# A planned attention and feed-forward kernel with batch 0's loads, its global rows and its whole order of work laid out anew

## The chip, the cores and the metric

The kernel runs on one core of a Trainium2 chip. The metric is the device time of one execution in microseconds (us). A core has TensorE (matmuls, into PSUM), VectorE, ScalarE and GpSimd, which work side by side, and SyncE, which here issues most of the loads. Each engine takes its instructions in the order in which the program lists them. In the profile they are called PE (and PEld for its weight loads), DVE, ACT, POOL and SP.

## The reference

Attention over 8 batches of 8 heads, 576 positions and 64 elements, in which each position sees its neighbours up to 32 away, 8 global positions are seen by all and see all; then a feed-forward layer on the 4608 tokens.

```python
scores = scale * np.matmul(q, k.transpose(0, 1, 3, 2))
mask = np.abs(pos[:, None] - pos[None, :]) <= window        # window = 32
mask = mask | is_global[:, None] | is_global[None, :]
scores = np.where(mask, scores, -1000000000.0)
scores = scores - np.max(scores, axis=-1, keepdims=True)
attn = np.exp(scores)
attn = attn / (np.sum(attn, axis=-1, keepdims=True) + 1e-09)
attn_out = np.matmul(attn, v)
x = np.ascontiguousarray(attn_out.transpose(0, 2, 1, 3)).reshape(B * S, H * D)   # 4608 x 512
h = x @ w_in                                                                      # 512 x 2048
g = np.maximum(h, 0.0) + np.log1p(np.exp(-np.abs(h)))
return g @ w_out                                                                  # 2048 x 512
```

## The kernel before

**Jobs and an order.** The kernel doesn't emit its instructions as its loops run. The loops add jobs to a planner (`_Order`, L20): a function that emits the instructions, what it costs on which engine, which jobs it needs, which buffers and PSUM banks it opens and uses. A tuple of some 1,720 numbers, `ORDER` (L335), then says in which order the jobs are placed and on which engine (job number times five plus engine). `run` (L179) goes along it with its own idea of times, gives each PSUM tile one of 8 banks and emits the jobs sorted by the planned start. The order that a job has on its engine is thus written out beforehand; the chip keeps to it and waits where a planned time isn't met. The planner's model has a wait of TensorE for its own instructions, in blocks of 256 with the first after 442 (`ASK`, `NEED`, `SLOW`, L38 to 41, `stall`, L44), and a rule for the port that VectorE and GpSimd share: a VectorE job marked `port` waits for the GpSimd job that is running (`self.other`, L217), a GpSimd job for the VectorE job of that kind (`self.mine`). Where TensorE would stand still for 0.7 us or more in the first 34 us, `keep` (L135) puts filler matmuls (L704, tile `warm`).

**Loads.** For batches 0 and 1, `add_parts` (L744) loads queries (w = 0) and keys (w = 1) in three pieces each, natural layout, on SP's queue: two of 256 positions (t = 0, 1) and a tail of 64 (t = 2, `FULL`). Each piece is cast to bf16, transposed by TensorE into PSUM (`tr`, L808), with matmuls beside it that pick out the global positions (tile `pick`), and copied out (`trev`, L833). Both halves of a piece share one PSUM tile. `fill` and `gev` (L865, L870) copy the picked keys and queries. Later batches are loaded whole (`load_qk`), cast, transposed by VectorE, and picked by matmuls (L849, L862). V comes in two halves of 4 loads each (`load_v`, L443), cast into `vb`. The first product's weights are loaded as four chunks by GpSimd's queue (L1304), between its casts. SP loads batch 1 after a marker that reads the second of these chunks (`follow`, L726), and V of batch 1 after one that reads the second chunk of the second product's weights. Those are issued by GpSimd (L1308) once its job `landed` (L1385) has copied an element of the last query piece of batch 1.

**Global rows.** Per batch, `sg` (L923) makes the scores of the 8 global queries against all keys, `mx` the maxima of both halves of the heads (L942, L943), `gexp` the exponentials (L949), `tpg` (L954, L956) their transposes, `ov` (L965) the product with V in 72 small matmuls into two PSUM tiles in turn. `odd` copies one of them to SBUF, `both` adds the other and takes the reciprocal of the sum, `gv` scales the result into `vg` for the values.

**Pairs, values, feed-forward.** The 36 `pairs` of 4 blocks of 32 positions are scored (`sc`, L1040), masked (in PSUM by a matmul for the first four, `mk` for the first two, else by VectorE, L1044), reduced to maxima (L1055, L1057), shifted (`sub`, L1063, on GpSimd or VectorE), exponentiated (L1076, L1080), summed (L1087, L1089), normalised (`no`, L1095, on GpSimd or VectorE) and transposed by VectorE (`tp`, L1104, tile `pt`). `val` (L1207, tile `xo`) multiplies with V. Four pairs make one of 9 tiles of 512 tokens (the first tile comes in three parts, the second in two) for the feed-forward layer: `first` (L1242, tile `h`), softplus (L1248), `second` (L1253, tile `o`), copy and store.

## Time and profile before

| | |
|---|---|
| time, median of 3 runs | 341.49 us (340.54 to 342.74) |
| time of the profiled execution | 342.18 us |
| its span, first to last instruction | 340.5 us |
| instructions | 12210 |
| busy TensorE, VectorE, ScalarE, GpSimd | 94%, 76%, 68%, 50% |
| moved by DMA | 42.74 MB |

A row of a timeline has the start in us from the begin of the span, the time in us, engine, line, operation, the tile written and the tiles read, shapes and count, and in brackets how long the engine stood idle before it and what ended that. "issue" is a wait for which the profile shows no releaser. A group has its busy time, the mean ns of one, and the idle time before its instructions. Of TensorE's time, "busy" counts overlapping matmuls once but includes the drain of each. A row of waits has who waited for whom, us in total, how often, and the longest. A row of a window has its length, then the busy time and the number of instructions of PE, PEld, DVE, ACT and POOL, the granted TensorE clock as a share of the full one, the busy share of the DMA engines and GB/s.

### The profile page before, as it was taken

What the parts mean: (1) busy time and instruction counts of PE and PEld (TensorE: products, weight loads), DVE (VectorE), ACT (ScalarE), POOL (GpSimd) and SP (SyncE); (2) the same over time, 40 slices, a digit from 0 to 9 for tenths busy, and PEclk for the clock granted to TensorE, in tenths of its full rate; (3) what the DMA queues carried; (4) which work ended last, traced back from release to release, by engine and by line L of the source; (5) the groups of instructions that cost most, each with busy time, mean ns of one, the idle gap of its engine ahead of it and who ended that gap; (6) DMA issues with size and microseconds to landing.
All of it is one profiled execution on the core that took longest, in us unless ns stands there. A gap on an engine that the chain in (4) does not pass through costs nothing.

```text
span 340.5 us, 12210 instructions
## 1 busy us (share of the span) xinstructions
PE 319.2 (94%) x5333; PEld 169.4 (50%) x5333; DVE 259.4 (76%) x409; ACT 230.0 (68%) x469; POOL 169.1 (50%) x155
## 2 busy tenths in 40 slices
PE   6787899988999999999799999999999989999996
PEld 3435785555555454544354445444544444445443
DVE  7598679994999799979999999799985979061000
ACT  5688789975687866489638583769466746765442
POOL 5464457863695789608375328644532431460000
PEclk9679999999999999999999999999999999999999
DMA  7999499979799999999950997008111020002003
GB/s 193 220 173 244 123 162 191 175 142 192 127 171 211 174 204 185 189 151 231 164 132 34 173 165 177 2 2 171 36 56 39 33 97 2 31 31 96 0 0 123
DMA packets 168733, 42.74 MB, mean 126 GB/s; under 512 B 153192, under 2 KB 165736, under 8 KB 168680
## 3 DMA queue, kind: packets, MB, share of 16 engines
q1 hardware_dynamic: 160664, 28.33, 47.4%
q0 software_dynamic: 6144, 10.49, 13.2%
q10 hardware_dynamic: 1872, 3.15, 2.5%
q8 instruction: 41, 0.67, 0.9%
q14 instruction: 12, 0.10, 0.1%
HBM read 36.71 MB, written 9.44 MB: 136 GB/s over the span
## 4 chain that ended last, share of the span: by engine, by line
PE 41%; DVE 23%; SPq 11%; POOL 7%; DMA 7%; issue 6%; ACT 4%; POOLq 0%; DVEq 0%; ACTq 0%
PE h L1242 19%; PE o L1253 15%; SPq L440 7%; SPq L445 4%; DMA stage<-in_q_dram 4%; DVE sm L1087 4%; PE xo L1207 3%; POOL pn L1095 3%; DVE st L1044 2%; DMA stage<-in_v_dram 2%; POOL st L1063 2%; PE s L1040 2%; DVE gm L942 2%; DVE m L1057 2%; DVE pn L1095 2%
## 5 line engine op out<-in xcount | busy, mean ns | idle before, releaser
L1253 PE MATMUL o<-wout,g 128*128 128x512 bf16 (+1 forms) x592 | 137.4, 374 | 0.0
L1242 PE MATMUL h<-xT,win 128*128 128x512 bf16 (+3 forms) x768 | 135.8, 326 | 0.4 <-DVE xT L696 0.2
L1248 ACT ACTIVATE g<-h 128x512 bf16<-128x512 f32 (+3 forms) x192 | 85.5, 501 | 44.8 <-PE h L1242 43.7
L1242 PEld LDWEIGHTS <-win 128*128 128x128 bf16 x768 | 67.3, 98 | 60.3 <-issue 1.2
L1253 PEld LDWEIGHTS <-g 128*128 128x128 bf16 x592 | 55.3, 98 | 60.7 <-ACT g L1248 1.3
L1063 POOL TENSOR_TENSOR st<-st,m 128x1024 f32<-128x1024 f32 x27 | 51.9, 1931 | 49.4 <-DVE m L1057 49.3
L1095 POOL TENSOR_TENSOR pn<-st,rs 128x1024 bf16<-128x1024 f32 (+1 forms) x29 | 51.4, 1783 | 48.5 <-DVE rs L1089 46.4
L1044 DVE TENSOR_TENSOR st<-s,mask 128x512 f32<-128x512 f32 x64 | 41.5, 676 | 12.0 <-PE s L1040 12.0
L1087 DVE TENSOR_REDUCE sm<-st 128x8 f32<-128x1024 f32 x32 | 38.3, 1197 | 8.6 <-ACT st L1080 8.6
L1057 DVE TENSOR_REDUCE m<-st 128x8 f32<-128x1024 f32 x32 | 38.4, 1207 | 0.4
L1080 ACT ACTIVATE st<-st 128x1024 f32<-128x1024 f32 x32 | 32.9, 1057 | 1.1 <-POOL st L1063 1.0
L1104 DVE STREAM_TRANSPOSE pt<-pn 128x512 int32<-128x512 int32 x36 | 24.6, 690 | 3.9 <-POOL pn L1095 3.6
L696 ACT CAST xT<-xo 128x512 bf16<-128x512 f32 (+3 forms) x31 | 12.9, 476 | 17.9 <-PE xo L1207 17.9
L696 ACT COPY osb<-o 128x512 f32<-128x512 f32 (+1 forms) x29 | 16.6, 577 | 11.1 <-PE o L1253 9.8
L1095 DVE TENSOR_TENSOR pn<-st,rs 128x1024 bf16<-128x1024 f32 (+1 forms) x11 | 19.9, 1818 | 0.1
L696 POOL CAST kb<-stage 128x1152 bf16<-128x1152 f32 (+2 forms) x12 | 14.4, 1218 | 8.1 <-DVE rs L1089 5.1
L949 ACT ACTIVATE pg<-sg,gnb 128x320 bf16<-128x320 f32 (+1 forms) x32 | 14.9, 575 | 5.0 <-DVE gnb L943 5.0
L693 POOL TENSOR_SCALAR qb<-stage 128x1152 bf16<-128x1152 f32 (+2 forms) x10 | 12.9, 1286 | 10.7 <-DMA stage<-in_v_dram 7.3
L1248 ACT ACT_TABLE_LOAD x13 | 16.7, 1283 | 0.5 <-PE h L1242 0.3
L1040 PE MATMUL s<-kx,qx 64*32 64x128 bf16 x1152 | 15.4, 224 | 1.3 <-DVE qx L789 0.6
L696 POOL CAST vb<-stage 128x1152 bf16<-128x1152 f32 x11 | 12.6, 1145 | 7.2 <-DMA stage<-in_v_dram 5.5
L1265 POOL DMA_DIRECT2D out_dram<-osb x24 | 14.0, 584 | 3.7 <-DVE osb L696 3.7
(124 smaller groups left out, 313.2 us busy)
## 6 DMA issues: line engine op xcount, KB each, us to landing
stage<-in_v_dram SPq DMA_DIRECT2D x64, 144.0 KB, 4.6
stage<-in_k_dram SPq DMA_DIRECT2D x48, 144.0 KB, 3.8
stage<-in_q_dram SPq DMA_DIRECT2D x48, 144.0 KB, 3.6
out_dram<-osb POOLq DMA_DIRECT2D x24, 256.0 KB, 3.2
out_dram<-osb ACTq DMA_DIRECT2D x11, 256.0 KB, 2.1
stage<-in_k_dram SPq DMA_DIRECT2D x4, 512.0 KB, 9.1
stage<-in_q_dram SPq DMA_DIRECT2D x4, 512.0 KB, 6.2
win<-in_moe_w_in_dram POOLq DMA_DIRECT2D x4, 512.0 KB, 6.9
```

Source lines behind the costliest of these rows:

```text
L440: eng.dma_start(out=stage[w][quad(r), :, e, :], in_=SRC[w][b, HG * g:HG * g + HG].rearrange("a (c i e) (f d) -> e f i (a c) d", i=BL, e=2, ...
L696: {"ACT": nc.scalar.copy, "DVE": V.tensor_copy, "POOL": nc.gpsimd.tensor_copy}[e](out, in_)
L1044: V.tensor_tensor(out=PS["st", n][:, h, :, :], in0=PS["s", n, h][:, :, :], in1=mask[:, h, j0:j0 + PB, :, :].rearrange("p j s i -> p j (s i ...
L1057: V.reduce_max(out=m[:], in_=flat(PS["st", n], h0, h1), axis=AX)
L1063: on(e).tensor_tensor(out=t, in0=t, in1=over(PS["m", n, y][:], SL * BL), op=OP.subtract)
L1080: nc.scalar.activation(out=t, in_=t, func=AF.Exp)
L1087: V.reduce_sum(out=sm[:], in_=flat(PS["st", n], h0, h1), axis=AX)
L1095: on(e).tensor_tensor(out=PS["pn", n][:, :, :, h0:h1].rearrange("p x s h -> p h x s"), in0=PS["st", n][:, h0:h1], in1=PS["rs", n, y][:].re ...
L1104: V.transpose(out=bass.AP(base.tensor, base.offset, ap=[list(base.ap[0]), [2 * STEP, PB // 2], [STEP + BL // 2, 2], [1, SL * BL]]), in_=PS ...
L1242: nc.tensor.matmul(out=h[:, :], lhsT=w_in_t[c // 4][:, kd, c % 4 * P:(c % 4 + 1) * P], rhs=PS["xT", m][:, kd, lo:hi], start=(kd == 0), sto ...
L1248: nc.scalar.activation(out=PS["g", m, c][:, lo:hi], in_=PS[key][:, lo_of(c, hi - lo)], func=AF.Softplus)
L1253: nc.tensor.matmul(out=PS["o", m, ns, a][:, :], lhsT=PS["g", m, kf][:, ns * P:(ns + 1) * P], rhs=w_out_t[kf // 4][:, kf % 4, a:z], start=( ...
```

## The change

The list of batch 0's pieces is written with the queries ahead; the global rows of batch 0 are reduced and exponentiated by halves of the heads, and their product with V goes into one PSUM tile, so that the copy and the sum of two are gone; each transposed half piece has a PSUM tile of its own; the marker ahead of the second product's weights reads the query tail of batch 1; the planner's port rule and several of its costs are changed; and `ORDER` is a new sequence.

```diff
-    SLOW = ((30000, 9300), (37000, 6500), (51000, 7300), (62000, 6500), (250000, 5600), (1e9, 4200))
+    SLOW = ((28000, 10700), (38000, 6700), (62000, 6500), (80000, 7200), (150000, 6200), (250000, 5800), (1e9, 4300))
+    def issue(self, j):
+        return j["moves"] or j["port"] == 2
+    def freed(self):
+        t = self.other[1]
+        for n, e in self.given[1:] if self.given else ():
+            if e != "POOL":
+                continue
+            j = self.jobs[n]
+            at = None if self.issue(j) or any(d["end"] is None for d in j["deps"] + j["behind"]) else self.due(j)
+            if at is None or at > t + 100:
+                break
+            t += j["cost"]["POOL"][0]
+        return t
-                    elif e == "DVE" and j["port"] and self.other[0] <= t + 100:
-                        t = max(t, self.other[1])
-                    elif e == "POOL" and not j["moves"]:
-                        t = max(t, self.mine)
+                    elif e == "DVE" and j["port"] and self.other[0] <= t + 100 and self.other[1] > t:
+                        t = self.freed()
+                    elif e == "POOL" and not self.issue(j) and t >= self.mine[0] - 1:
+                        t = max(t, self.mine[1])
...
     ORDER = (
-        42, 107, 121, 126, 47, 52, 92, 116, 9, 236, 221, 225, 240, 87, 132, 137, 83, 14, 251, 255, 97, 143, 102, 268,
+        24, 42, 47, 52, 83, 4, 191, 121, 126, 107, 92, 208, 195, 210, 102, 298, 111, 19, 97, 132, 137, 29, 116, 152,
...
-    FIRST = ([(0, 0), (1, 0), (1, 1), (1, 2), (0, 2), (0, 1)], [(0, 0), (1, 0), (1, 1), (1, 2), (0, 2), (0, 1)])
+    FIRST = ([(0, 0), (0, 2), (0, 1), (1, 0), (1, 2), (1, 1)], [(0, 0), (1, 0), (1, 1), (1, 2), (0, 2), (0, 1)])
...
-            if e == 0:
-                PS["tr", b, w, t] = psum(("tr", b, w, t), [P, 2, HG, P], BF16)
-            ps = PS["tr", b, w, t]
+            ps = PS["tr", b, w, t, e] = psum(("tr", b, w, t, e), [P, HG, P], BF16)
...
-                for y in range(2):
+                for y in range(2 if b else 1):
                     PS["ov", b, y] = psum(("ov", b, y), [P, 2 * D + 1], FP32)
...
-            t = PS["odd", b]
-            V.tensor_tensor(out=t[:], in0=PS["ov", b, 0][:, :], in1=t[:], op=OP.add)
+            t = PS["odd", b] if b else PS["ov", 0, 0]
+            if b:
+                V.tensor_tensor(out=t[:], in0=PS["ov", b, 0][:, :], in1=t[:], op=OP.add)
...
-        heads = ((0, 1),)
+        heads = ((0, 1),) if b else ((0,), (1,))
...
-            job = o.add({"POOL": (1040, 1040), "DVE": (1000, 1080)} if n < TP else {"POOL": (1905, 1905), "DVE": (1130, 1210)}, lambda e, y=y: no(e, y), [job], rank=at,
+            job = o.add({"POOL": (1040, 1040), "DVE": (650, 730)} if n < TP else {"POOL": (1905, 1905), "DVE": (1130, 1210)}, lambda e, y=y: no(e, y), [job], rank=at,
...
-            T["landed"] = o.add(pool(100), lambda e: nc.gpsimd.tensor_copy(seen[:, 0, :], natural(0, 1)[:, 0, 0, 0, 0:1]), [T["part", 1, 0, FULL]], rank=0)
+            T["landed"] = o.add(pool(100), lambda e: nc.gpsimd.tensor_copy(seen[:, 0, :], natural(0, FULL)[:, 0:1]), [T["part", 1, 0, FULL]], rank=0)
```

In the new sequence SP's first loads are: the key tail of batch 0, its first query piece, its two key pieces, the query tail, the second query piece, V, then two key pieces of batch 1, the marker for the first weights, and the rest of batch 1 with its last query piece at the end. TensorE's list has 22 filler matmuls instead of 29, none of them between the global row of batch 0 and the pairs behind it. On VectorE stand 4 normalisations and 9 subtractions of the later pairs (before: 8 and 5), on GpSimd the others.

60 lines of the change are left out of this document (33 added, 27 removed), and 142 rows, old and new, of the table ORDER.

## The prediction

> **What bounds the kernel now.** I read the page first, then who waited for whom, then the chain of waits, and last the timelines of the stretches that these pointed at.
>
> ```profile
> PE 319.2 (94%) x5333; PEld 169.4 (50%) x5333; DVE 259.4 (76%) x409; ACT 230.0 (68%) x469; POOL 169.1 (50%) x155
> PE   6787899988999999999799999999999989999996
> DVE  7598679994999799979999999799985979061000
> PEclk9679999999999999999999999999999999999999
> ```
>
> TensorE is the engine that is never far from busy, but VectorE stands at nine tenths in most slices from the 7th to the 30th, so attention is paced by VectorE, and TensorE fills up with the feed-forward matmuls. How much of TensorE's time is work shows in the two groups of the feed-forward part and one stretch of the chain in which they run with no wait:
>
> ```profile
> L1253 PE MATMUL o<-wout,g 128*128 128x512 bf16 (+1 forms) x592 | 137.4, 374 | 0.0
> L1242 PE MATMUL h<-xT,win 128*128 128x512 bf16 (+3 forms) x768 | 135.8, 326 | 0.4 <-DVE xT L696 0.2
> ...
> 294.33 4.10 PE o L1253 x19
> ```
>
> 19 matmuls in 4.10 us are 0.216 us each. Both products have 576 full matmuls' worth of columns (36 or 144 groups by the loops), 1152 in all, so 1152 x 0.216 = 249 us of the span cannot be ordered away. What is left, some 91 us, is attention's own matmuls, the start, and waits. The change leaves the matmuls of both products as they are, so it can only move the last two. The waits of TensorE that name a releaser are led by two VectorE results, the transposed probabilities and the transposed global rows:
>
> ```profile
> PE xo L1207 <- DVE pt L1104: 3.4, 3, 1.6
> PE ov L965 <- DVE pgt L956: 3.2, 4, 2.0
> ```
>
> **The order and the port.** Behind those two lines stand VectorE instructions that take far longer than others of their kind. First VectorE, then GpSimd in the same stretches, then TensorE just behind them:
>
> ```profile
> 68.16 2.67 DVE L1095 TENSOR_TENSOR pn<-st,rs 128x1024 bf16<-128x1024 f32 x1
> 158.50 5.75 DVE L1095 TENSOR_TENSOR pn<-st,rs 128x1024 bf16<-128x1024 f32 x1
> 179.83 1.30 DVE L1095 TENSOR_TENSOR pn<-st,rs 128x1024 bf16<-128x1024 f32 x1
> 183.41 4.35 DVE L696 CAST vb<-stage 128x1152 bf16<-128x1152 f32 x1
> 189.53 0.75 DVE L696 CAST vb<-stage 128x1152 bf16<-128x1152 f32 x1
> 273.14 2.51 DVE L1095 TENSOR_TENSOR pn<-st,rs 128x1024 bf16<-128x1024 f32 x1
> ```
>
> ```profile
> 157.87 1.52 POOL L693 TENSOR_SCALAR qb<-stage 128x1152 bf16<-128x1152 f32 x1
> 159.28 3.79 POOL L1063 TENSOR_TENSOR st<-st,m 128x1024 f32<-128x1024 f32 x2
> ...
> 183.81 1.91 POOL L1063 TENSOR_TENSOR st<-st,m 128x1024 f32<-128x1024 f32 x1
> 185.65 1.49 POOL L696 CAST kb<-stage 128x1152 bf16<-128x1152 f32 x1
> ```
>
> ```profile
> 72.22 0.38 PE L1207 MATMUL xo<-pt,vg 32*64 32x384 bf16 x8 [1.63 <-DVE pt L1104]
> 169.34 0.80 PE L965 MATMUL ov<-vb,pgt 32*32 32x129 bf16 x72 [1.97 <-DVE pgt L956]
> 277.28 0.40 PE L1207 MATMUL xo<-pt,vg 32*64 32x448 bf16 x8 [1.23 <-DVE pt L1104]
> ```
>
> The same normalisation takes 1.30 us alone and 5.75 us while GpSimd runs three instructions without a pause; it ends 1.2 us after the last of them. The V cast that takes 0.75 us alone ends after GpSimd's second instruction. The excess is 1.37 + 4.45 + 1.21 us on the three normalisations and 3.60 us on the cast, 10.6 us of VectorE, and TensorE waits 1.63 + 1.97 + 1.23 = 4.83 us right behind the three. The old plan lets a VectorE job of this kind wait only for the GpSimd job that is running at that moment (`other`); the new one (`freed`) counts the whole run of GpSimd jobs that are due behind it, which is what the rows show. So the new sequence is laid out with the price that these rows have. It doesn't avoid the exposure: by the instruction lists, VectorE still has 13 normalisations and subtractions of the later pairs (8 and 5 before, 4 and 9 after) and 8 instead of 10 of the later casts. I take three fifths of the 4.83 us: **-2.9 us**, between -4.8 (all gone) and +1.0 (one new collision of the size of the last). Without a collision, the next to arrive at these places is the exponential or the score matmul that feeds the same chain, for which I leave the other two fifths.
>
> The Trainium skill (SBUF — State Buffer, "Who interferes with whom") says that VectorE and GpSimd share one port pair under an exclusive lock, held "for the whole instruction" by whichever starts first. By that the 5.75 us would have been one GpSimd remainder of 0.89 us and 1.30 us of its own, and the cast at 183.41, which started before GpSimd's at 183.81, would not have waited. The rows differ: VectorE got in only when GpSimd had nothing more queued. By the page `freed` would count too much, and this term would shrink to about -1.
>
> **The start.** The words of the change promise that batch 0's queries are loaded ahead of its keys. The list of loads does not show it: `ORDER` overrides `FIRST`. Before: keys 0, keys 1, queries 0, key tail, query tail, queries 1. After: key tail, queries 0, keys 0, keys 1, query tail, queries 1. The first four are the same bytes, so they are in at the same time; what differs is what follows them.
>
> ```profile
> 11.83 0.42 PE L823 MATMUL tr<-ident,kb 64*64 64x64 bf16 x8 [1.04 <-POOL kb L696]
> 13.31 0.29 PE L1040 MATMUL s<-kx,qx 64*32 64x128 bf16 x2
> 18.48 0.68 PE L932 MATMUL sg<-kx,qg 64*32 64x320 bf16 x16 [0.76 <-DVE qg L696]
> 19.10 2.90 PE L704 MATMUL warm<-pgt 128*128 128x512 bf16 x7
> 28.88 0.25 PE L1207 MATMUL xo<-pt,vg 32*64 32x128 bf16 x4 [1.49 <-issue]
> 30.17 3.73 PE L1242 MATMUL h<-xT,win 128*128 128x128 bf16 x64 [0.20 <-DVE xT L696]
> ```
>
> ```profile
> 10.55 0.76 POOL L615 TENSOR_SCALAR mask<-near 128x144 bf16<-128x144 f32 x2 [0.95 <-DVE mask L611]
> 11.38 0.40 POOL L696 CAST kb<-stage 128x256 bf16<-128x256 f32 x1
> ...
> 24.19 0.80 POOL L1304 DMA_DIRECT2D win<-in_moe_w_in_dram  x1
> ```
>
> ```profile
> win<-in_moe_w_in_dram POOLq DMA_DIRECT2D x4, 512.0 KB, 6.9
> ```
>
> Before, the key tail stood on GpSimd behind the mask (10.55 + 0.76), so its transposes began at 11.83 and the first scores at 13.31. After, it is cast ahead of the mask, and the mask is finished at about the same time, so the first scores can start some 0.5 us sooner. The queries' last transposes now stand ahead of the second pair's scores, so that the global row (18.48) can follow those scores at once: some 1.5 us sooner. The path then reaches the issue wait at 28.88. The kernel's planner books such waits at TensorE's 442nd instruction and every 256 after it, each released some 10 us after the instruction 312 places earlier; for the 698th, which is the one at 28.88, that is the 386th, the end of the global row, so this wait moves with it. But the first feed-forward matmuls (30.17) need all four weight chunks, the last of which is issued at 24.19 and, at the page's median of 6.9 us to landing (its last column), is in at about 31, and ScalarE has eight exponentials to do whatever their order. I take **-1.0 us**, between -2.0 and 0.
>
> ```profile
> 24.42 0.60 DVE L696 COPY odd<-ov 64x129 f32<-64x129 f32 x2
> 25.66 0.28 DVE L982 TENSOR_TENSOR odd<-ov,odd 128x129 f32<-128x129 f32 x1
> ```
>
> One sum for batch 0's global rows drops these, 0.88 us of VectorE ahead of the first values. The issue wait up to 28.88 hides them: **0 us**, and if that cover goes, up to -0.9. The maxima by heads add one reduction and let the exponential start on half a row; a bank for each turned piece adds no instruction and holds PSUM banks until its copy is done: both 0, and I let neither be worth more than those 0.9 us, lost or gained.
>
> **The weights of the second product.** Their loads stand on GpSimd behind a marker (`landed`): so far a copy out of batch 1's last query piece, now one out of its query tail.
>
> ```profile
> 35.06 0.61 POOL L696 CAST kb<-stage 128x512 bf16<-128x512 f32 x1 [0.70 <-DMA stage<-in_k_dram]
> 41.02 0.23 POOL L1385 COPY seen<-stage 128x1 f32<-128x1 f32 x1 [3.33 <-DMA stage<-in_q_dram]
> ```
>
> ```profile
> 75.97 4.53 DMA stage<-in_q_dram
> ...
> 82.90 0.46 PE L849 MATMUL pick<-qb,pick 128*32 128x128 bf16 x18 [1.02 <-POOL qb L693]
> ```
>
> The marker waited 3.33 us at 41.02; without that, and with batch 1's keys issued before the marker of the first weights instead of behind it, these weights start 3 to 6 us sooner. SP's queue stands behind them, up to the query load that ends TensorE's wait of 1.02 us at 82.90. That wait goes: **-1.0 us**, at most -1.0; it gains nothing more, since TensorE has feed-forward work there.
>
> **Sum.** The profiled execution took 342.2 us (span 340.5). -2.9 - 1.0 - 1.0 = -4.9 gives 337.3; the median of the runs lies 0.7 under the profiled one, so 336.6 us. The rest of the new sequence, whose waits the old trace can't show, I take at 0 and put into the range.
>
> **Rivals.**
> *The collisions move instead of going.* The plan's times drift from the chip's by some tenths of a microsecond per step, and 13 exposed instructions are left. For it: the old sequence was planned with a port rule too, and has four collisions. Against: that rule ignored the queue behind. Then only the start and the load are gained, and one new wait of 1 us comes: 342.2 - 2.0 + 1.0 - 0.7 = 340.5 us.
> *The clock stays low.*
>
> ```profile
> 11.35:21.59 10.24, 8.71 (x138) 4.25 (x139) 8.12 (x17) 7.57 (x31) 5.86 (x8) 0.50 1.26 186
> ```
>
> From 11.35 to 21.59 the granted clock was 0.50, and it came back under the seven filler matmuls of 19.10. After, these stand only ahead of the first values. If the clock comes back behind the 64 feed-forward matmuls, their 3.73 us become up to 7.5 and the gain of the start is lost: 336.6 + 3.7 = 340.3 us. For it: TensorE was busy 8.71 of those 10.24 us and still slow. Against: the same seven fillers stand just ahead of these 64. The Trainium skill (TensorE: Matmul & The Clock Gate, "Part 1: The HAM clock gate") has the full clock come after about 3.4 us of sustained work; by that rule the clock should have risen well before 21.59, which this row does not bear out.
> *Early keys push the first weights back: slower.* In the new list SP issues two of batch 1's key pieces behind V, ahead of its marker for the first weights; before, the two went out here, and SP's issue itself was held up for 5.31 us:
>
> ```profile
> 26.40 5.31 SPq L490 DMA_DIRECT2D stage<-in_k_dram  x2
> ```
>
> Those two pieces took until 35.06 and later to arrive, with the weights on the other queue. If the weights yield instead, the last chunk is some 4 to 5 us later, near 35.5. It decides from the moment when the 10th of the 16 first groups needs that chunk, about 31.3: 4.2 us of waiting, the gain of the start gone, no later cover, and the collisions of the next 40 us laid out for other times: 342.2 + 4.2 - 0.7 = 345.7 us. Against it: the key rows waited for the weights, not the reverse. The Trainium skill (DMA: Bandwidth & Descriptors, "Queues, rings and completion order") has each DMA engine alternate between queues packet by packet, which is this rival's mechanism; the 8.7 us from 26.40 to 35.06 speaks more for the weights going first.
>
> **Chances.** Forecast 0.55, moved collisions 0.26, low clock 0.07, weights pushed back or another new wait of that size 0.12. About 1% (3.4 us) is what a measurement can tell here. Under 338.1 us lie most of the forecast's cases (0.48) and few of the rest (0.03): faster 0.51. Over 344.9 us lie the last rival and a tail of the second (0.15). Between: 0.34. The forecast alone runs from 332.5 (every term at its lower end, and 1 us of further waits gone) to 339.5; eight in ten over all cases from 332.5 to 343.5, which leaves out most of the last rival.
>
> **What would show it.** Right, if VectorE's normalisations and V casts have no member over 2 us, the waits of TensorE for pt and pgt fall to 3 us together, the first 64 feed-forward matmuls start before 29.5 us, and the marker is copied before 37 us. Wrong, if the granted clock is 0.50 past 28 us, if TensorE waits for the first weights, or if new waits of 2 us stand in the chain beyond 100 us.

## The result, and the profile after

| | before | after |
|---|---|---|
| median of the runs, us | 341.61 (4 runs, 340.54 to 342.74) | 350.63 (4 runs, 349.16 to 351.72) |
| profiled execution, us | 342.18, span 340.5 | 349.62, span 347.9 |
| mean granted TensorE clock | 0.985 | 0.975 |

The ratio is 1.0246, with a 95% interval of 1.0206 to 1.0286: 8.4 us slower by the ratio (9.0 by the medians), where 5 us faster was forecast. The page of the changed kernel:

```profile
PE 314.6 (90%) x5278; PEld 171.5 (49%) x5326; DVE 263.2 (76%) x418; ACT 226.0 (65%) x455; POOL 170.1 (49%) x156
...
PEclk9669999999999999999999999999999989999999
...
win<-in_moe_w_in_dram POOLq DMA_DIRECT2D x4, 512.0 KB, 9.9
```

TensorE's share went from 94 to 90%. (48 of its matmul records are missing here, 5278 beside 5326 weight loads, so counts of matmuls in this one trace run a little low.) The clock row has an 8 late in the span, where before had only 9s there. The weights of the first product took a median of 9.9 us to land, before 6.9. SP's queue and its first loads:

```profile
1.25 1.37 SPq L510 DMA_DIRECT2D stage<-in_k_dram  x2
2.67 0.60 SPq L506 DMA_DIRECT2D stage<-in_q_dram  x1
...
16.33 3.25 SPq L506 DMA_DIRECT2D stage<-in_k_dram  x2
```

The two loads of the key tail went first, so the first large piece was issued at 2.67 us, before at 1.27. At 16.33 batch 1's two key pieces go out, just when GpSimd issues the weights. TensorE in order of time (the bracket is the wait ahead of a row, and what ended it):

```profile
14.47 0.63 PE L1061 MATMUL s<-kx,qx 64*32 64x128 bf16 x32
...
19.51 0.38 PE L1055 MATMUL s<-mask,ident 128*128 128x512 bf16 x1 [1.05 <-ACT st L1097]
22.59 0.58 PE L1055 MATMUL s<-mask,ident 128*128 128x512 bf16 x1 [2.71 <-DVE rs L1110]
...
32.64 1.74 PE L1263 MATMUL h<-xT,win 128*128 128x128 bf16 x28 [0.64 <-DMA win<-in_moe_w_in_dram]
35.56 1.74 PE L1263 MATMUL h<-xT,win 128*128 128x128 bf16 x28 [1.18 <-DMA win<-in_moe_w_in_dram]
...
87.84 0.35 PE L863 MATMUL pick<-qb,pick 128*32 128x128 bf16 x12 [1.46 <-DVE qb L707]
...
246.23 1.02 PE L1228 MATMUL xo<-pt,vb 32*64 32x32 bf16 x100
249.65 0.22 PE L1228 MATMUL xo<-pt,vb 32*64 32x64 bf16 x4 [2.41 <-issue]
...
276.52 0.42 PE L1061 MATMUL s<-kx,qx 64*32 64x128 bf16 x32
279.09 1.03 PE L980 MATMUL ov<-vb,pgt 32*32 32x129 bf16 x72 [2.16 <-DVE pgt L970]
```

The first scores come at 14.47 instead of 13.31. The second bank of the fourth pair's scores is that of a turned query piece whose copy VectorE makes only at 21.82, hence the 2.71 us. The weights hold TensorE twice. Far behind that stand two waits that before did not have: 2.41 us inside a run of value matmuls, ended by nothing that the profile shows ("issue"), and 2.16 us for `pgt` at the last global product. What made the second shows on VectorE and GpSimd:

```profile
266.50 3.75 POOL L1116 TENSOR_TENSOR pn<-st,rs 128x1024 bf16<-128x1024 f32 x2 [4.54 <-DVE rs L1110]
270.19 1.33 POOL L1286 DMA_DIRECT2D out_dram<-osb  x2
271.52 1.16 POOL L712 CAST vb<-stage 128x1152 bf16<-128x1152 f32 x1
...
269.06 1.80 DVE L712 CAST vb<-stage 128x1152 bf16<-128x1152 f32 x1
270.78 2.98 DVE L1084 TENSOR_TENSOR st<-st,m 128x1024 f32<-128x1024 f32 x1
...
278.58 0.45 DVE L970 TENSOR_REDUCE pgt<-own 128x288 bf16<-128x288 bf16 x1
```

VectorE's V cast (0.75 us alone) and its subtraction end 0.6 and 1.1 us after GpSimd lets go, at 270.25 and 272.68. The subtraction waited through two output stores and a cast. All of pgt's chain stands behind it. The windows behind the two waits (PE busy and its count first, the granted clock third from the right):

```profile
246.83:250.24 3.41, 1.00 (x112) 0.87 (x103) 0.24 (x1) 0.12 (x1) 1.89 (x1) 1.00 0.05 12
...
277.55:280.96 3.41, 1.53 (x74) 1.12 (x76) 2.96 (x7) 0.78 (x3) 2.88 (x2) 0.76 0.23 82
280.96:284.37 3.41, 3.41 (x13) 1.25 (x11) 1.03 (x4) 1.55 (x3) 0.87 (x1) 0.74 0.16 59
```

TensorE is busy 1.00 and 1.53 of 3.41 us. The clock of 0.76 and 0.74 is one stretch that lies across both windows: from 279.3 to 282.7 us the granted clock was 0.50. Before, every window from 240 us on had 1.00.

### The profile page after: what moved, and what is told of

The parts are those of the page before. It is cut to its first block, busy times and chain, and to the rows that moved or that the text cites. A ratio compares the mean times of both kernels' runs of the same rounds, so it can differ in the third digit from the quotient of the medians.

```text
span 347.9 us, 12155 instructions
## 1 busy us (share of the span) xinstructions
PE 314.6 (90%) x5278; PEld 171.5 (49%) x5326; DVE 263.2 (76%) x418; ACT 226.0 (65%) x455; POOL 170.1 (49%) x156
## 4 chain that ended last, share of the span: by engine, by line
PE 63%; DVE 16%; issue 6%; DMA 5%; SPq 4%; POOL 4%; ACT 2%; DVEq 0%; POOLq 0%
PE h L1263 29%; PE o L1274 25%; DVE st L1065 4%; PE xo L1228 3%; DMA win<-in_moe_w_in_dram 3%; DVE m L1078 3%; POOL pn L1116 2%; PE s L1061 2%; DVE sm L1108 2%; SPq L461 2%; DMA stage<-in_v_dram 2%; DVE st L1084 1%; PE ov L980 1%; SPq L510 1%; SPq L506 1%
## 5 line engine op out<-in xcount | busy, mean ns | idle before, releaser
L1274 PE MATMUL o<-wout,g 128*128 128x512 bf16 (+1 forms) x553 | 130.4, 375 | 3.7 <-issue 2.9
L1116 POOL TENSOR_TENSOR pn<-st,rs 128x1024 bf16<-128x1024 f32 (+1 forms) x33 | 60.7, 1848 | 82.5 <-DVE rs L1110 74.0
L1084 POOL TENSOR_TENSOR st<-st,m 128x1024 f32<-128x1024 f32 x23 | 43.4, 1896 | 37.3 <-DVE m L1078 37.2
L1065 DVE TENSOR_TENSOR st<-s,mask 128x512 f32<-128x512 f32 x64 | 40.8, 677 | 10.9 <-PE s L1061 10.8
L712 DVE CAST xT<-xo 128x512 bf16<-128x512 f32 (+3 forms) x23 | 11.9, 558 | 13.2 <-PE xo L1228 13.2
L712 ACT CAST xT<-xo 128x512 bf16<-128x512 f32 (+3 forms) x25 | 11.0, 487 | 14.4 <-PE xo L1228 14.4
L1061 PEld LDWEIGHTS <-qx 64*32 64x32 bf16 x1152 | 10.6, 92 | 15.5 <-issue 14.1
L1084 DVE TENSOR_TENSOR st<-st,m 128x1024 f32<-128x1024 f32 x9 | 17.1, 1911 | 0.1
L1228 PE MATMUL xo<-pt,vb 32*64 32x96 bf16 (+2 forms) x1328 | 14.2, 210 | 2.4 <-issue 2.4
```

Of the source, the lines that this page charges most:

```text
L712: {"ACT": nc.scalar.copy, "DVE": V.tensor_copy, "POOL": nc.gpsimd.tensor_copy}[e](out, in_)
L1061: nc.tensor.matmul(out=PS["s", n, g][quad(a ^ g), x, :], lhsT=qx[b % 2][rows(g), a, j * BL:(j + 1) * BL], rhs=kx[b % 2][rows(g), a, e0 * B ...
L1065: V.tensor_tensor(out=PS["st", n][:, h, :, :], in0=PS["s", n, h][:, :, :], in1=mask[:, h, j0:j0 + PB, :, :].rearrange("p j s i -> p j (s i ...
L1084: on(e).tensor_tensor(out=t, in0=t, in1=over(PS["m", n, y][:], SL * BL), op=OP.subtract)
L1116: on(e).tensor_tensor(out=PS["pn", n][:, :, :, h0:h1].rearrange("p x s h -> p h x s"), in0=PS["st", n][:, h0:h1], in1=PS["rs", n, y][:].re ...
L1228: nc.tensor.matmul(out=PS["xo", v_, hd // 2][hd % 2 * D:(hd % 2 + 1) * D, (x - X0) * BL:(z - X0) * BL], lhsT=lhs, rhs=rhs, start=start, st ...
```

## The experiments

Each ratio is to the kernel before, run on the same chip in turn with it. The old kernel's own median moved from 341.02 to 342.73 us between the sets of runs, so two rows are better compared by their ratios than by their medians, and a difference of two ratios has the uncertainty of both. Where an expectation names a wait of 2.37 us, it counts the whole gap beyond the usual step between two matmuls; the row's bracket has 2.16 for the same one. The edits that move work use a helper on the finished list of jobs: `behind(a, b)` puts job a right behind job b, `behind(a, b, 0)` right ahead of it; an engine's own instructions keep their order otherwise.

| run | median, us | ratio (95% interval) |
|---|---|---|
| the change | 350.63 | 1.0246 (1.0206 to 1.0286) |
| e1 marker first | 352.57 | 1.0304 (1.0242 to 1.0367) |
| e2 old kernel, early keys | 340.91 | 0.9960 (0.9922 to 0.9999) |
| e3 turned piece early | 350.92 | 1.0256 (1.0197 to 1.0314) |
| e4 key tail second | 349.47 | 1.0220 (1.0156 to 1.0284) |
| e5 global product later | 347.41 | 1.0167 (1.0084 to 1.0250) |
| e6 six matmuls ahead | 349.48 | 1.0211 (1.0144 to 1.0277) |
| e7 four edits of the start | 351.27 | 1.0249 (1.0177 to 1.0322) |
| e8 e5, e6 and e7 | 346.66 | 1.0119 (1.0055 to 1.0183) |
| e9 e4, e5, e6 and two fills | 346.65 | 1.0178 (1.0145 to 1.0212) |
| e10 GpSimd's cast first | 347.31 | 1.0207 (1.0173 to 1.0242) |
| e11 old kernel, covers | 340.21 | 0.9972 (0.9937 to 1.0007) |
| e12 old kernel, early keys and covers | 339.01 | 0.9948 (0.9919 to 0.9977) |
| e13 new code, old order | 340.94 | 0.9965 (0.9930 to 0.9999) |
| e14 new start, old rest | 360.93 | 1.0531 (1.0466 to 1.0596) |
| e15 old start, new rest | 343.83 | 1.0057 (1.0016 to 1.0098) |
| e16 seven more fillers | 346.34 | 1.0120 (1.0036 to 1.0205) |
| e17 e13, early keys and covers | 341.94 | 0.9964 (0.9916 to 1.0012) |
| e18 e15 and e5 | 342.61 | 1.0001 (0.9963 to 1.0038) |

### The first theory: early keys push the weights back (e1, e2)

The new trace showed the slower rival of the prediction at work to the letter: the last weight chunk landed at 35.51 us. So the first two runs took it out of the new kernel and put it into the old.

```diff
-                if x == 0 and b:
+                if b and (w, t) == (1, 0):
                     follow(0, w_in_t[1])
```

> The changed kernel, with the marker of the first weights put ahead of batch 1's first key piece again, so that no key load of batch 1 starts before the weights. Theory A (the early keys push the first weights back, and TensorE's wait for them is most of the loss of 9 us): the last chunk of w_in lands by about 32 us instead of 35.5, the waits of TensorE for win (1.8 + 2 + 1.2 by the trace) go, and the time falls by 3 to 4 us, to about 347. Theory B (the late copy of a turned piece, with the half clock, costs the start 2 to 2.5 us) and C (the key tail's loads at the head of SP's queue cost 1.2 to 1.4 us): less than 1 us either way, because the feed-forward matmuls then wait for something else. Theory D (the loss is in the rest of the sequence): less than 1 us either way.

```diff
+    behind(T["part", 1, 1, 0], T["part", 1, 0, 0], 0)
+    behind(T["part", 1, 1, 1], T["part", 1, 0, 0], 0)
```

> The kernel before, with batch 1's first two key pieces put ahead of the marker of the first weights, as the changed kernel has them; nothing else moves. Theory A: the chunks of w_in land 3 to 5 us later than at 21.6 to 30.7, TensorE waits for them, and the time rises by 3 to 4 us, to about 345. Theories B, C and D, which put the loss elsewhere: within 1 us of 341.6, since the key rows were not on TensorE's path.

e2 refutes it. e1 gained nothing either, but it is the weaker test: in its trace the last chunk still landed at 34.26 us, since GpSimd issued it behind a normalisation that waits for VectorE. TensorE's waits for the weights fell from 1.8 to 0.5 us all the same, and a new wait of 1.6 us for `pt` stood right behind. e2's page and its row on TensorE show that the mechanism is real:

```profile
win<-in_moe_w_in_dram POOLq DMA_DIRECT2D x4, 512.0 KB, 10.6
```

```profile
31.81 4.45 PE L1242 MATMUL h<-xT,win 128*128 128x128 bf16 x40 [3.40 <-DMA win<-in_moe_w_in_dram]
```

The weights landed in a median of 10.6 us instead of 6.9, and TensorE waited 3.40 us. Yet the time did not rise. By the trace's records the 129th matmul of the first product started at 50.1 us instead of 47.0, but the 321st at 108.7 instead of 108.0: the lag of 3.1 us shrank to 0.7, because the old kernel's waits for its queries (1.02 us at 82.90) and for `pt` at 71 us (1.63, in e2 0.51) took it up.

### Bank and queue head (e3, e4), and four edits of the start (e7)

```diff
+    behind(T["turn", 0, 0][1][0], T["gev", 0])
```

> The changed kernel, with the copy out of one turned piece of the queries (the one whose bank the fourth pair's second half waits for, at 21.8 us) put ahead of the first sum of the global rows on VectorE. Theory B: the waits of 1.05 and 2.71 us of the fourth pair's mask matmuls go, and the time falls by about 2 us, to 348.6. Theory A: the feed-forward matmuls still wait for the weights that come at 35.5 us, so less than 0.7 us is gained. Theories C and D: less than 0.7 us.

```diff
+    behind(T["part", 0, 1, 2], T["part", 0, 0, 0])
```

> The changed kernel, with the loads of batch 0's key tail issued behind the first query piece instead of at the head of SP's queue. Theory C: the first query piece is issued at about 1.3 us instead of 2.67, the first scores start 1.2 us sooner than 14.5, and the time falls by about 1.2 us. Theory A: the start is sooner by that much, but the feed-forward matmuls wait for the weights all the same, so less than 0.5 us of it reaches the end. Theories B and D: less than 0.5 us.

e3 took the 2.71 us from the mask matmuls and met it again as a wait of 3.10 us at the first global product:

```profile
19.14 0.59 PE L1055 MATMUL s<-mask,ident 128*128 128x512 bf16 x2 [1.05 <-ACT st L1097]
...
23.18 2.14 PE L980 MATMUL ov<-vb,pgt 32*32 32x129 bf16 x72 [3.10 <-ACT st L1097]
```

e4 did what theory C said: first scores at 12.99 us, and 1.2 us sooner by the records all the way to 225 us; the span fell by 1.4 us. The ratio fell by 0.0026 (0.9 us), which the intervals do not separate from none. Then the edits together, with the last weight load ahead of the normalisations (it is `o.jobs[15]`, the load before it `o.jobs[14]`):

```diff
+    behind(T["turn", 0, 0][1][0], T["gev", 0])
+    behind(T["part", 0, 1, 2], T["part", 0, 0, 0])
+    behind(o.jobs[15], o.jobs[14])
-                if x == 0 and b:
+                if b and (w, t) == (1, 0):
```

> The changed kernel with four edits of the start together: batch 1's first keys behind the marker of the first weights, the key tail's loads behind the first query piece, the turned piece copied out early, and the last of the four weight loads issued on GpSimd ahead of the two normalisations instead of behind them. Theory S (weights, bank and head of SP's queue hide one another, so that each edit alone gains little): the last chunk of w_in lands by 32 us, TensorE waits under 1 us for win, the first feed-forward matmul starts by 29.5 us, the 129th by 49.5 instead of 52.8, and the time falls by 3 us or more. Theory L (what is gained there is lost again in the following 40 us): the 129th is early, but the time falls by less than 1.5 us.

```profile
30.84 3.73 PE L1263 MATMUL h<-xT,win 128*128 128x128 bf16 x64 [0.47 <-ACT xT L712]
36.86 0.32 PE L1228 MATMUL xo<-pt,vg 32*64 32x256 bf16 x8 [2.29 <-DVE pt L1125]
```

The 64 matmuls now run without a wait for weights, whose last chunk landed at 32.02. Then 2.29 us for `pt` stand where the weights stood, and the "issue" wait at 49 us grew to 2.5. Nothing was gained, as in theory L, and sooner than it has it: the 129th matmul of the first product, which both theories put early, started at 54.8 us (52.8 in the change). Several chains that end close together at 36 us are the likely reason; no run shows it by itself.

### The two late waits (e5, e6, e10) and e8

Job 1463 is the last global product, the others are second-product matmuls that stand behind it; in e6 job 1300 is the value matmuls at 246 us; in e10 job 1458 is GpSimd's cast, 1426 the normalisation ahead of its stores.

```diff
+    for n in (1352, 1353, 1369, 1370, 1372, 1373, 1374, 1375, 1376, 1377):
+        behind(o.jobs[n], o.jobs[1463], 0)
```

> The changed kernel, with ten matmuls of the second product that stand right behind the last global product on TensorE put ahead of it, four of them from the two groups that are open. Theory D1 (the late wait of 2.37 us for pgt at 276.7, which a subtraction of 2.98 us and a V cast of 1.80 us on VectorE make, and the half clock of 3.4 us that follows it, are 2.4 to 4 us of the loss): the wait falls to under 0.7 us, no window of half clock stands at 279, and the time falls by 2 to 4 us. Theory D0 (TensorE is not on the path there; the ten matmuls were done in time anyway): within 0.7 us. What happens before 270 us stays as it is.

```profile
276.54 2.11 PE L1274 MATMUL o<-wout,g 128*128 128x512 bf16 x9 [0.16 <-issue]
278.58 0.80 PE L980 MATMUL ov<-vb,pgt 32*32 32x129 bf16 x72
```

The wait is gone, the product takes 0.80 us instead of 1.03, and the window from 277.55 has the clock at 1.00: theory D1. The medians are 3.2 us apart, the ratios 0.0079 (2.7 us), and their intervals still overlap.

```diff
+    for n in (1180, 1198, 1181, 1182, 1199, 1200):
+        behind(o.jobs[n], o.jobs[1300], 0)
```

> The changed kernel, with six matmuls of the second product that stand behind the value matmuls at 246.1 us put ahead of them. Theory F (the wait of 2.41 us at 249.65, for which no semaphore is late, is TensorE's own instruction stream: in every trace such a wait stands at the same count of matmuls and weight loads, 8641 here, and ends 8.8 to 9.1 us after the 312th before it): the wait stays at the 8641st, so six value matmuls earlier in their run, ends at the same time, and shrinks by about 1.2 us, to 1.2; the time falls by 1.2 us, more if a half clock behind it goes. Theory N (it is a hidden wait of those value matmuls for data): the wait stays between the same two value matmuls.

```profile
247.21 0.98 PE L1228 MATMUL xo<-pt,vb 32*64 32x32 bf16 x94
249.33 0.24 PE L1228 MATMUL xo<-pt,vb 32*64 32x96 bf16 x9 [1.14 <-issue]
```

94 value matmuls instead of 100 ahead of the wait, and 1.14 us instead of 2.41: theory F in both its numbers. The wait keeps its place in the count of instructions, not among the data. The median fell by 1.2 us, within the noise; 0.90 us came back at 251 us as a wait for `xT`.

```diff
+    behind(o.jobs[1458], o.jobs[1426])
```

> The changed kernel, with GpSimd's V cast at 271.52 us put ahead of the two output stores that it issues at 270.19 us. Theory P (VectorE's subtraction at 270.78 us took 2.98 us instead of about 1.2 because GpSimd's next work followed the stores at once, so that a run of GpSimd work with stores in it holds VectorE to its end): the cast then ends by about 271.4, the subtraction by about 272.6 instead of 273.76, and the wait of TensorE for pgt falls from 2.37 to about 1.2 us; the time falls by 1.2 us, and by up to 1.7 more if the half clock behind the wait goes. Theory Q (the subtraction is slow by itself, or by the stores): it keeps its 2.9 us, and the time stays within 0.7 us.

```profile
270.10 1.67 POOL L712 CAST vb<-stage 128x1152 bf16<-128x1152 f32 x1
271.71 1.12 POOL L1286 DMA_DIRECT2D out_dram<-osb  x2
...
270.69 2.16 DVE L1084 TENSOR_TENSOR st<-st,m 128x1024 f32<-128x1024 f32 x1
```

```profile
278.17 0.80 PE L980 MATMUL ov<-vb,pgt 32*32 32x129 bf16 x72 [1.34 <-DVE pgt L970]
```

The subtraction fell from 2.98 to 2.16 us and the wait from 2.16 to 1.34, as theory P has it to within 0.4 us. It also fits turns: GpSimd's cast, ready when its normalisation ended, took 1.67 us instead of 1.16, and VectorE's waiting cast ended in between, at 270.76. The ratio fell by 0.0039 (1.3 us), within the two intervals.

e8 is e5, e6 and e7 together:

> The changed kernel with all six edits: the four of the start, the ten matmuls ahead of the last global product, and the six ahead of the value matmuls at 246 us. If the three places are independent, their gains add: 3 + 2.4 to 4 + 1.2, so 342 to 344 us, about the time of the kernel before. If the collisions on VectorE shift with the start, new waits come and less than 4 us is gained.

346.66 us, a gain of 4 where 6.6 to 8.2 was expected. By the ratios e8 gained 4.3 us, and e5 and e6 alone 2.7 and 1.2: the start's four edits gave next to nothing here either.

### Filling the early waits (e9)

On top of e4, e5 and e6, with job 351 the scores at 46 us and 369 those at 52:

```diff
+    for n in (228, 243, 244, 315, 316, 317):
+        behind(o.jobs[n], o.jobs[351], 0)
+    for n in (279, 280, 281, 282, 283):
+        behind(o.jobs[n], o.jobs[369], 0)
```

> The changed kernel with five covers of TensorE's waits together: the key tail's loads behind the first query piece; the ten matmuls ahead of the last global product; the six ahead of the value matmuls at 246 us; and, new, three groups of the first product and three matmuls of the second (2.3 us of work) ahead of the scores at 46 us, and five matmuls of the second (1.1 us) ahead of the scores at 52 us, where TensorE waits 1.2 to 2.7 and 0.8 to 1.4 us at the 1473rd and 1729th of its instructions. Theory F (those are waits for TensorE's own instructions, and filled for nothing): they fall by 1.2 to 2 and by about 1 us, and the time to 343 to 345 us. Theory L (what is gained in the first 60 us comes back as another wait): 345 to 346.5, no better than the first three covers alone would give (1.2 + 3 + 1.2 off 350.6).

```profile
48.51 1.03 PE L1263 MATMUL h<-xT,win 128*128 128x256 bf16 x8 [1.53 <-ACT g L1269]
...
51.38 2.31 PE L1263 MATMUL h<-xT,win 128*128 128x256 bf16 x28 [0.50 <-DVE st L1065]
```

Both "issue" waits vanished from the trace, and in their place TensorE waited 1.53 us for ScalarE. 346.65 us: theory L again. By the ratio the gain is only 2.3 us, less than e8's 4.3.

### Covers in the old kernel (e11, e12)

Jobs 952 and 1123 are the global products at 167 and 202 us, 1298 the value matmuls at 242.

```diff
+    for n in (865, 866, 867, 877, 878, 879, 880, 881, 882, 883, 884):
+        behind(o.jobs[n], o.jobs[952], 0)
+    for n in (1043, 1044, 1045):
+        behind(o.jobs[n], o.jobs[1123], 0)
+    for n in (1180, 1211):
+        behind(o.jobs[n], o.jobs[1298], 0)
```

> The kernel before, with TensorE's own waits of 2.13 us (global product at 167 us), 0.90 us (global product at 202 us) and 0.75 us (value matmuls at 242 us) covered by eleven, three and two matmuls of the second product that stand behind them. If such waits are on the path to the end, as the ten matmuls showed for the changed kernel: 2 to 3 us less, 339 to 340.5. If they are given back in the following stages: within 1 us of before.

> The kernel before, with the early keys of batch 1 and with the same covers. The early keys alone gave 0.996 [0.992, 1.000]. If both gains add: 337.5 to 340 us, under both kernels. If the early keys' gain was noise: as with the covers alone.

e12 adds e2's two lines. The covers took the waits away, but e11's median gained 0.8 us, less than the 2 to 3 expected and not separated from nothing; its profiled execution, span 335.7 us, was its fastest. e12's 2.0 us lie in its range, and at 0.9948 it is half a per cent faster than the kernel before, with an interval that ends below 1.

### Order or code, start or rest (e13 to e15)

The old order needs more than eight PSUM banks if each turned piece has its own, so e13 and e15 go back to two pieces to a bank and to the old order of the first pieces. All three also take back a small change of what `fill` and `sg` wait for in the planner (left out below). In all three the planner takes the next job of whichever engine can go on, with each engine's list as given. The lists, with n the place of the second batch's global scores:

```diff
-    FIRST = ([(0, 0), (0, 2), (0, 1), (1, 0), (1, 2), (1, 1)], [(0, 0), (1, 0), (1, 1), (1, 2), (0, 2), (0, 1)])
+    FIRST = ([(0, 0), (1, 0), (1, 1), (1, 2), (0, 2), (0, 1)], [(0, 0), (1, 0), (1, 1), (1, 2), (0, 2), (0, 1)])
-            ps = PS["tr", b, w, t, e] = psum(("tr", b, w, t, e), [P, HG, P], BF16)
+            if e == 0:
+                PS["tr", b, w, t] = psum(("tr", b, w, t), [P, 2, HG, P], BF16)
+            ps = PS["tr", b, w, t][:, e]
-    o.follow(NEW)
+    o.follow(OLD)
```

```diff
+    start = NEW[:n]
+    o.follow(start + [x for x in OLD if job(x) not in jobs(start)])
```

for e14, and with OLD and NEW exchanged for e15.

> The changed kernel's code (one sum and maxima by heads for batch 0's global rows, the second product's marker behind the query tail) with the old order of the work on every engine, and, since the old order does not fit otherwise, with two turned pieces to a bank as before. Theory O (the loss is in the order): about 341 to 343 us, as before or a little under. Theory K (the code costs too): 344 us or more.

> The changed kernel with its own order up to the second batch's global scores (about the first 58 us) and the old order, with its engines, from there on. Theory O1 (the start loses 4 us by the count of TensorE's waits, and the new order of the rest loses the other 4 to 5): 345 to 347 us, and the two late waits of 2.4 us are not there. Theory O2 (all of the loss is in the rest): 341 to 343. Theory O3 (all of it is in the start): 349 or more.

> The other way about: the old order (and its banks) up to the second batch's global scores, the new order from there on. Theory O1: 345 to 347 us, with the waits of 2.4 us at about 245 and 274 us still there. Theory O2: 349 or more. Theory O3: 341 to 343.

e13 settles the first question: with the old order the changed code is no slower than before (0.9965). The loss is in the order. e15 settles most of the second: the old start with the new rest is 1.0057, so 1.9% of the 2.46, some 6.5 us, hang on the first 58 us of the list. Its trace has no wait in the value matmuls at 245 us, which theory O1 had expected to stay; the wait for `pgt` stayed (2.15 us). e14 does not mirror it: at 1.0531 it is worse than either, through a seam that neither kernel has (its trace shows one wait of 6.5 us for `pt` at 80 us), where 345 to 347 us and no late waits were expected. It is telling all the same beside e13. The same old rest, the same run of value matmuls, in e13 and then in e14:

```profile
241.61 1.05 PE L1170 MATMUL xo<-pt,vb 32*64 32x32 bf16 x104
242.46 0.29 PE L1170 MATMUL xo<-pt,vg 32*64 32x128 bf16 x8
242.54 0.53 PE L1170 MATMUL xo<-pt,vb 32*64 32x64 bf16 x40
```

```profile
258.54 1.05 PE L1168 MATMUL xo<-pt,vb 32*64 32x32 bf16 x104
259.39 0.29 PE L1168 MATMUL xo<-pt,vg 32*64 32x128 bf16 x8
259.47 0.40 PE L1168 MATMUL xo<-pt,vb 32*64 32x64 bf16 x21
261.99 0.28 PE L1168 MATMUL xo<-pt,vb 32*64 32x96 bf16 x19 [2.12 <-issue]
```

Behind the old start no wait, behind the new one 2.12 us. One thing that a start leaves behind for 240 us later is a count of instructions: the new one has fewer filler matmuls, 22 against 29 in the old kernel and 34 in e13 and e15.

### The count of fillers (e16), and two last versions (e17, e18)

```diff
         count = int((t1 - t0) * self.FILL / 220)
+        count += {14: 2, 7: 5}.get(count, 0)
```

> The changed kernel with seven more filler matmuls, 29 as before: two behind the first 14, where TensorE waits for its first cast, and five behind the seven ahead of the first values. Theory C (the count of instructions decides where a late block of instructions falls, and with it the wait of 2.4 us at about 247 us): that wait goes or is under 1 us, and the time falls by 1.5 to 3 us. Theory T (something else in the start, its timing or its loads, decides): the wait stays at the 8641st instruction with 2 us or more, and the time stays within 1 us, or rises by up to 1 us for the five fillers.

```profile
246.73 1.05 PE L1229 MATMUL xo<-pt,vb 32*64 32x32 bf16 x104
247.58 0.30 PE L1229 MATMUL xo<-pt,vg 32*64 32x128 bf16 x8
247.66 0.53 PE L1229 MATMUL xo<-pt,vb 32*64 32x64 bf16 x40
```

Theory C. Seven matmuls that compute nothing, all ahead of 31 us, and the wait at 247 us is gone; the median fell by 4.3 us, to 1.0120 (by the two intervals a gain of 1 to 7.5 us), where 1.5 to 3 was expected. In the profiled executions the wait is the whole difference: TensorE goes on behind its place at 249.65 us in the change and 247.5 in e16, reaches the last global product at 279.09 and 277.02, and the spans are 347.9 and 345.8 us. The other 2.2 of the median lie within the intervals, or in the half clock that followed the wait in other profiles of the new start, as in e1:

```profile
246.83:250.24 3.41, 1.07 (x84) 0.96 (x83) 0.33 (x1) 0.24 (x1) 1.74 (x1) 0.75 0.00 0
250.24:253.65 3.41, 3.41 (x24) 1.20 (x9) 3.41 (x6) 3.07 (x4) 0.00 (x0) 0.50 0.02 5
253.65:257.07 3.42, 3.42 (x13) 1.39 (x12) 3.38 (x5) 1.60 (x4) 0.32 (x1) 0.75 0.00 0
```

The three windows hold one stretch at half clock, from 248.6 to 255.4 us, in which TensorE was busy for 6.2 of 6.8 us; by that its work there took some 3 us longer (an estimate: half of 6.2). Two of the change's four runs have a mean clock of 0.970 and 0.971 and took 351.6 and 351.7 us, the two at 0.975 took 349.2 and 349.6; e16's four have 0.975 to 0.985.

What TensorE waits for is in the trace too. The page counts the blocks of a queue that it calls instruction:

```profile
q8 instruction: 41, 0.67, 0.8%
```

These are blocks of 16 KB, and every late wait of this kind ends 1.2 to 1.6 us behind one of them. In the change the 33rd block starts at 247.14 us and is in at 248.39, and TensorE goes on at 249.65; in e16 it starts at 242.75 and is in at 244.15, before TensorE gets there at 247.5. In the eleven traces with 22 fillers this block starts 6.1 to 6.4 us behind the instruction 312 places ahead of the wait, in the nine with 29 or 34 only 1.5 to 2.3 us. So the wait is for a block of instructions whose transfer starts late. Why the fillers change that is open: in e16 the 8641st instruction lies only seven matmuls earlier in the same run of value matmuls, and as in the change it is reached 6.2 us behind the 312th before it.

e17 has e13's code, e2's two lines and e11's covers (by the new numbers); e18 has e15 and e5's edit.

> The changed kernel's code with the old order and banks, with batch 1's early keys and with the covers of TensorE's three waits at 167, 202 and 242 us. Old order alone gave 0.9965, early keys alone 0.996, covers alone 0.997. If the three add: 0.990, about 338.5 us. If they share one slack: 339 to 341, as the old kernel with early keys and covers gave (0.9948).

> The old order up to the second batch's global scores, the new one behind it, and the ten matmuls of the second product put ahead of the last global product. The old start with the new rest gave 343.8 (1.0057). If the late wait of 2.37 us at 272 us is what the new rest costs: 341 to 342, about the kernel before. If not: 343 to 344.5.

e18: the last global product no longer waits, and the ratio is 1.0001. As far as the runs tell, the new rest costs nothing beyond its late wait, and gains nothing either; the intervals of e15 and e18 overlap. e17 at 0.9964 adds nothing to its parts. e12 keeps the lowest ratio, but the intervals of e2, e11, e13 and e17 overlap its own.

## Why the prediction was wrong

**The sum's last line, "The rest of the new sequence, whose waits the old trace can't show, I take at 0", is the step that failed**, and with it the treatment of the issue wait in the term for the start ("this wait moves with it"). I knew that such waits stand at a fixed count of TensorE's instructions, and followed one of them, at 28.88 us, for the gain of 1 us. I did not ask what would become of the other boundaries once seven fillers had gone. In every run whose start has 22 fillers TensorE waits at 247 us, or at the same place of the program, for 2.1 to 2.4 us (0.7 to 1.1 where six matmuls were put ahead); in none with 29 or 34 does it. In the complete traces it is the 8641st matmul or weight load. The price of the missing fillers is e16's 4.3 us, 2.1 of it seen in the profiled executions. Asking where the boundary falls would not have been enough: in e16 it falls among the same matmuls, and only its block of instructions comes sooner.

**"Order and port" (-2.9, at worst +1.0).** The rule was to gain by ending VectorE's waits for GpSimd's runs. There is no normalisation of 5.75 us any more (the longest on VectorE took 1.80), but nine subtractions on VectorE took 1.91 us on average where the shortest took 1.17, one query cast 2.54, and the collision at 270.78 made the late wait that e18 prices at 1.9 us (1.0057 to 1.0001, with intervals that overlap). That `freed` foresees a run's end was the argument; but it stops counting at an output store, and on the chip the cast behind the stores held the subtraction too. The skill rule that I had weighed there, one instruction's remainder at most (the Trainium skill, SBUF — State Buffer, "Who interferes with whom"), does not give 2.98 us either; e10's turns, one instruction each, do agree with it. Part of the term's gain came: the old kernel waited 1.97 us for `pgt` at 169 us, and the new one has no wait of 0.7 us or more between 90 and 247 us.

**"Start" (-1.0).** The first scores came 1.2 us later, not 0.5 sooner. I had seen the key tail's two loads go first on SP and put that at nothing: "The first four are the same bytes, so they are in at the same time". But SP issues them one behind the other, and the two loads of 64 KB took its first 1.4 us, ahead of all three pieces of 512 KB. In e4 the first four are the same bytes too, with one large piece ahead of the tail, and the first scores start at 12.99 instead of 14.47; the ratio gives 0.9 us for it, within the noise. What is left of the first stretch (6.5 less 4.3 less 0.9, so 1.3 us, less than the uncertainty of any of the three) I can only put down to the weights, the bank and `pt`: e1, e3 and e7 could not part them.

**One sum, maxima by heads (0).** Right within its bounds: e13 has both, and the new marker, and is 1.2 us faster by its ratio, 0 to 2.4 by its interval. **A bank for each piece (0).** It made the wait of 2.71 us; by e3 that wait alone is worth nothing at the end.

**"The weights of the second product" (-1.0).** Their issue began at 40.27 instead of 41.19 us, not 3 to 6 us sooner. The marker no longer waited for a load, but GpSimd came to it late: two normalisations ahead of it (30.51 and 34.66 us) had waited 3.10 and 3.11 us for VectorE. The queries did land sooner (the last at 73.5 us, before at 80.5), but TensorE's wait for them stayed (1.46 us at 87.84): the cast behind the load lasted 2.54 us beside GpSimd.

**The rivals.** The one that ended on the slower side had its mechanism and its landing time right (35.5 us, measured 35.51), not its size (4.2 us of waiting, measured 1.8; 345.7 us, measured 350.63), and was still not the cause: e2. Its error is the sentence "no later cover": e2 shows 2.4 of 3.1 us given back by 108 us. The Trainium skill's rule on shared queues (DMA: Bandwidth & Descriptors, "Queues, rings and completion order") fits e2's 6.9 to 10.6 us. The low clock came, but at 279 us, behind the new wait, not at 28: the granted clock was back at 1.00 from 26.8 us.

**What was to show it.** A V cast of 2.14 us on VectorE at 194 us (none over 2 was to be right), waits for pt and pgt of 3.5 us together (3 or less), the first 64 feed-forward matmuls at 31.40 (before 29.5), the marker at 40.15 (before 37), a wait for the first weights, and waits of 2 us beyond 100 us: all four signs of "right" failed, and two of "wrong" came.

## What to carry to other kernels

A change of how many instructions an engine issues can make a wait far from the edit: look for "issue" waits in the whole new trace, and hold the blocks of the instruction queue beside them. Here seven fillers took one such wait away (e16), and six longer matmuls put ahead of the run of short ones halved it (e6); no run gives a rule by which either could be planned. Price a wait only after asking what later slack takes it up (e2), and what stands right behind it (e3, e7, e9). An order by a planner is as good as its model of what one engine does to another: exchange start and rest of two orders, as e15 and e18 did, before explaining either.

## What the runs showed of the hardware

- A wait of TensorE for its own instructions depends on the count of matmuls and weight loads so far: in complete traces all such waits of 0.8 us or more stood at counts 7 or 8 above 442 plus a multiple of 256 (the count takes in the few semaphore records on TensorE's queue; without them 8641 is 8634, exactly 442 and 32 times 256), and those of the new start at 8641 ended 8.8 to 9.1 us after the 312th before in e1, e3 and e4. In the old kernel the 8641st was passed 6.7 us after it without a wait, in e16 6.2, so the latency is not one number. The block of 16 KB on the instruction queue that such a wait is for started 6.1 to 6.4 us after the 312th before in the runs that waited there and 1.5 to 2.3 in those that did not; what delays it is open.
- One wait of 2.4 us can take the clock with it, and need not: of the eleven profiles with the wait at 247 us (262 in e14) seven show a granted clock of 0.50 for 3.4 or 6.8 us behind it, the change's own and those of e5, e8 and e9 none. Behind the wait for `pgt` at 277 us the change has 0.50 for 3.4 us, e4 and e6 with the same wait (2.15 us) none.
- The median of the old kernel moved from 341.02 to 342.73 us between sets of runs, and single runs of one kernel in one set by 1.5% and more; gains under 1 us were not to be told here even with ten runs.
